# Sixteen attention heads without folded softmax weights, and the sign of 64-bit weights by ScalarE's leaky rectifier

## The chip, the cores and the metric

The kernel runs on one core of a Trainium2 chip. It uses TensorE (PE in the profile), VectorE (DVE), ScalarE (ACT), GpSimd (POOL) and the DMA queue that SyncE (SP) issues. The metric is the device time of one execution in microseconds (us): the median of 3 runs.

## The reference

Three layers follow one another; `rel` is query position minus key position.

```python
# attention: B, H, S, D = 4, 8, 576, 64, window 128
scores = q @ k.T / sqrt(D)
scores = where((rel >= 0) & (rel < 128), scores - slope[h] * abs(rel), -1e9)
attn = softmax(scores);  x = (attn @ v) as [B, S, 512]
# gated layer, d_ff 1024
h = gelu_tanh(x @ w_in);  u, v = halves of h
v_s = w_sg @ (layernorm(v) * g_ln) + b_sg
x = x + (u * v_s) @ w_out
# token-shift layer
xk, xr = mu_k * x + (1 - mu_k) * x_prev, mu_r * x + (1 - mu_r) * x_prev
out = sigmoid(xr @ w_r) * (max(xk @ w_k, 0) ** 2 @ w_v)
```

w_in, w_out, w_k, w_v and w_r come as 64-bit floats; everything else is fp32.

## The kernel before, in words

**Order of work.** There are 32 heads (4 batches of 8). Heads 0 to 7, with the decoding of w_in, come first (slots 0 to 8 of the loop over `slot(n)`). Then each batch's gated layer (`moe1(b)`) is interleaved with the attention of the next batch's heads, by the costs that are written beside the steps: heads 8 to 15 with `moe1(0)`, heads 16 to 23 with `moe1(1)`, heads 24 to 31 with `moe1(2)`. `moe1(3)` runs with the decoding of w_k, and `phase2` is the token-shift layer. All operations are recorded first. A list scheduler with a cost model then gives each engine its fixed order; where an operation has several possible engines ("adp" is ACT, DVE or POOL) it also picks the engine, and tables of offsets (`PRI`, `ENG`) shift priorities. So an operation that vanishes moves others, also from one engine to another.

**A head.** Its 576 queries make 4 tiles of 128 and one of 64. A query tile i sees the key blocks i-1 and i, 256 columns in all, of which the causal window leaves 128 for each query. `s_bank` multiplies queries and keys (tile `s`, PSUM); from head 8 on this takes fp32r copies `QK` of the input `rawqk` and the rest `KL` that they leave. `s_tile` adds bias and mask on DVE (L680, the output `p` and its extreme `nmax`), takes the exponential on ACT (L399), folds, and scales by the reciprocal sum `rin` (L472, L475 or L482, on DVE, POOL or ACT).

**Fold.** Keys outside the window have weight 0 after the exponential. In the key block i-1 the columns right of the diagonal are left, in block i those up to it. `fold(n)` (`n >= FOLD`, FOLD = 0: every head) adds the two 128-column halves into one (`p<-p`, L419 on DVE or L421 on POOL). `tf_step` transposes the four folded tiles in one go (tile `tf`, L385), copies them to `pf` (L407 or L409), and two triangular masks part them again into the two key halves (`keep`: L438 on POOL, L445 on DVE). `tf4_step` does this for the fifth tiles of two heads. `av_step` then multiplies v with the parts (tile `a`).

**64-bit weights.** `job` loads 128 rows of a weight as pairs of 32-bit words. ACT scales the high word in place (`st<-st` or `wraw<-wraw`, L399). On DVE the maximum of that and of its multiple by -2^32 deals with the sign (`wdec<-st` or `wdec<-wraw`, L455); a shift and a merge with the low word follow (L472, L455 with two inputs). The fp32 result `wdec` is split into an fp32r high part (ACT, DVE or POOL) and what it leaves (DVE or POOL). There are 36 such jobs: 8 of w_in, 8 of w_out, 8 of w_k, 4 of w_r, 8 of w_v. `wdec` has 4 buffers for w_in, 2 for w_out, and 1 for w_k, w_r and w_v.

Of the kernel before, what the change touches and what calls it, by code (L numbers as in the profile page):

```python
# [9 lines left out]
F32 = mybir.dt.float32  # L10
# [3 lines left out]
ACTF = mybir.ActivationFunctionType  # L14
ALU = mybir.AluOpType
# [5 lines left out]
P = 128  # L21
# [19 lines left out]
    ("xg", "dve/pool", "dve"): 4000,  # L41
}
NWARM = 10
FOLD = 0
FM = (1, 1)


# [32 lines left out]
class Vw:  # L80
# [25 lines left out]
    def real(self):  # L106
        t = self.base
        if t.real is None:
            t.real = t.rec.open_pool(t.pool).tile(list(t.shape), t.dtype, tag=t.tag, name=t.name, bufs=t.bufs)
        a = t.real  # L110
        for k, x in self.ops:
            if k == "ix":
                a = a[x]
            elif k == "bc":
                a = a.bitcast(x)
            elif x == 3:
                a = a.rearrange("p a b -> p (a b)")
            elif x == 4:
                a = a.rearrange("p a b c -> p (a b c)")
        return a  # L120
# [374 lines left out]
def attn_gmlp_rwkv_kernel(  # L495
# [18 lines left out]
    nc = tc.nc  # L514
    K = Build(nc)
# [11 lines left out]
    def T(pool, shape, dtype, tag, name=None, bufs=None):  # L527
        return R.tile(pool, shape, dtype, tag, name or tag, bufs)

    xs = [T("dr", [P, NC, S + 1], F32, f"xs{b}") for b in range(B)]  # L530
    ident = T("attc", [P, P], F32, "ident")
# [12 lines left out]
    def job(dst_h, dst_l, src, n, dup=False, raw=None, dec=("wraw", "wdec")):  # L544
        if src.dtype != F32:
            if raw is None:
                raw = T(stage[0][0], [P, n, 2], U32, stage[0][1], "wraw")
            K.dma(raw.flat()[:, 0:2 * n], src.bitcast(U32), P * n * 8)
            lo, hi = raw[:, :n, 0], raw[:, :n, 1]
            w = T(dec[0], [P, n], F32, dec[1], "wdec", bufs=4 if dec[0] == "tp" else (2 if dec[0] == "wraw" else 1))  # L550
            wu = w.bitcast(U32)
            hf = hi.bitcast(F32)
            K.act(hf, hf, ACTF.Copy, scale=2.0 ** -112)
            K.stt(w, hf, -(2.0 ** 32), hf, ALU.mult, ALU.max)
            K.ts(wu, wu, 3, None, ALU.logical_shift_left, None)
            K.stt(wu, lo, 29, wu, ALU.logical_shift_right, ALU.bitwise_or, cost=68 + n / 0.96)
        else:
            w = T(stage[0][0], [P, n], F32, stage[0][1], "wraw")
            if dup:
                K.dma(w[0:64], src, 64 * n * 4)  # L560
                K.dma(w[64:128], src, 64 * n * 4)
            else:
                K.dma(w, src, P * n * 4)
        K.copy(dst_h, w, "adp")
        K.sub(dst_l, w, dst_h)
# [8 lines left out]
    def sg_job(kk, half):  # L574
        c = slice(half * HS, half * HS + HS)
        src = w_sgT[kk * P:min(S, kk * P + P), c]
        job(w_sg_t[:, kk, 0, c], w_sg_t[:, kk, 1, c], src, HS, dup=kk == 4)

    def out_job(kk, half):
        c = slice(half * 256, half * 256 + 256)  # L580
        job(w_out_t[:, kk, 0, c], w_out_t[:, kk, 1, c], cols(w_out, kk, half), 256)

    x_t = {}
    NH = B * H
    rawqk, rawv, QK, KL, VS, PT, SUM, PTc = {}, {}, {}, {}, {}, {}, {}, {}

    def plain_s(n):
        return n in PLAIN_S

    def fold(n):  # L590
        return n >= FOLD

    def plain_a(n):
        return n in PLAIN_A
# [114 lines left out]
    def t1_step(n):  # L709
        if fold(n):  # L710
            return tf_step(n)
        t = T("psT", [P, 4, P], F32, "t")
        K.transposes([(t[:, j, :], PT[n, i][:, c:c + P], ident)
                      for j, (i, c) in enumerate(((0, 0), (1, 0), (1, P), (2, 0)))])
        if plain_a(n):
            pf = T("pt", [P, 4, P], F32, "ph1", "pf1")
            K.copy(pf, t)
            PTc[n, 0] = pf
            return
        ph = T("pt", [P, 4, P], F32R, "ph1")  # L720
        pl = T("pt", [P, 4, P], F32R, "pl1")
        K.copy(ph, t)
        K.sub(pl, t, ph)
        PTc[n, 0] = (ph, pl)

    def tf_step(n):

        t = T("psT", [P, 4, P], F32, "t", "tf")
        K.transposes([(t[:, j, :], PT.pop((n, j)), ident) for j in range(4)])
        pf = T("pt", [P, 7, P], F32, "ph1", "pf")  # L730
        if n % FM[0] < FM[1]:
            K.copy(pf[:, 0:4, :], t)
            K.keep(pf[:, 4:7, :], pf[:, 1:4, :], True, "dp")
            K.keep(pf[:, 0:4, :], pf[:, 0:4, :], False, "dp")
        else:
            K.keep(pf[:, 4:7, :], t[:, 1:4, :], True, "d")
            K.keep(pf[:, 0:4, :], t, False, "d")
        PTc[n, 0] = pf

    def tf4_step(n):  # L740
        t = T("psT", [P, 2, 64], F32, "t", "tf4")
        K.transposes([(t[:, j, :], PT.pop((n + j, 4)), ident[:64, :64]) for j in range(2)])
        pf = T("pt", [P, 2, 2, 64], F32, "pf4")
        if n % FM[0] < FM[1]:
            K.copy(pf[:, 0], t)
            K.keep(pf[:, 1], pf[:, 0], True, "dp")
            K.keep(pf[:, 0], pf[:, 0], False, "dp")
        else:
            K.keep(pf[:, 1], t, True, "d")
            K.keep(pf[:, 0], t, False, "d")  # L750
        PTc[n, 1] = pf

    def t2_step(n):
        if fold(n):
            if n % 2:
                tf4_step(n - 1)
            return
        t = T("psT", [P, 4, P], F32, "t")
        o4 = 0 if plain_s(n) else 64
        K.transposes([(t[:, j, :], PT[n, i][:, c:c + P], ident)  # L760
                      for j, (i, c) in enumerate(((2, P), (3, 0), (3, P)))] +
                     [(t[:, 3, 0:64], PT[n, 4][:64, o4:o4 + 128], ident[:64, :64]),
                      (t[:, 3, 64:128], PT[n, 4][:64, o4 + 64:o4 + 192], ident[:64, :64])])
        for i in range(5):
            PT.pop((n, i))
        if plain_a(n):
            pf = T("pt", [P, 4, P], F32, "pl1", "pf2")
            K.copy(pf, t)
            PTc[n, 1] = pf
            return  # L770
        ph = T("pt", [P, 2, P], F32R, "ph2")
        pl = T("pt", [P, 2, P], F32R, "pl2")
        pf = T("pt", [P, 2, P], F32, "pf")
        K.copy(ph, t[:, 0:2, :])
        K.sub(pl, t[:, 0:2, :], ph)
        K.copy(pf, t[:, 2:4, :])
        PTc[n, 1] = (ph, pl, pf)
# [64 lines left out]
    def slot(n):  # L842

        steps = []
        cur, prev = n < NH, n - 1
        has = prev >= 0

        def add(c, f, *a):
            steps.append((c, lambda: f(*a)))
        if cur:  # L850
            add(440, s_bank, n, (0, 1))
        if has:
            add(0, prep_v, prev)
            add(480, t1_step, prev)
        if has:
            add(490, t2_step, prev)
        if cur:
            add(440, s_bank, n, (2, 3))
        if has and prev % 2:
            add(2100, av_step, prev - 1)  # L860
        if cur:
            add(220, s_bank, n, (4,))

            def tail():
                prep_head(n + 1)
                load_head(n + 2)
                load_v(n + 1)
            add(0, tail)
        return steps
# [129 lines left out]
    def phase2(w_k_t):  # L999
# [42 lines left out]
        for kk in range(NC):  # L1042
            job(w_r_t[:, kk, 0, :], w_r_t[:, kk, 1, :], rows(w_r, kk), DM, dec=("raw2", "wdec"))
# [185 lines left out]
```

## Time and profile before

| | |
|---|---|
| median of 3 runs | 627.09 us (625.8 to 627.79) |
| the profiled execution's own time | 628.37 us |
| its span, first to last instruction | 626.6 us |
| mean granted TensorE clock, share of full speed | 0.977 |
| busy: PE, DVE, ACT, POOL | 95%, 76%, 56%, 30% |

Of the columns of the profile: an engine's busy time is followed by the number of its instructions (x). PEclk is the clock granted to TensorE as a share of 2.4 GHz (its lower level, 1.2 GHz, is 0.50). Ends of matmuls are modelled, so a busy PE can still be waiting a little.

### The profile page before, as it was taken

The page shows a single profiled execution, that of the slowest core. Times are in us where ns is not written, and L with a number is a line of the kernel's source. Part 1 is how long each engine was busy: PE and PEld are TensorE (multiplying, and loading weights), DVE is VectorE, ACT ScalarE, POOL GpSimd, SP SyncE. Part 2 cuts the span into 40 slices and gives each one's busy share as a digit, 9 for nine tenths or more (in the row PEclk, how much of TensorE's full clock was granted, in tenths as well). Part 3 has the DMA queues.
Part 4 walks back from the last instruction along what each step waited for, and adds up shares of the span by engine and source line. Part 5 has one row for each costly group of instructions (what it writes and reads, how often), then busy time and mean ns, then how long its engine had stood idle before and what let it go on. Part 6 is the DMA issues. An engine that isn't in the chain of part 4 may idle for free.

```text
span 626.6 us, 10161 instructions
## 1 busy us (share of the span) xinstructions
PE 595.6 (95%) x3458; PEld 498.7 (80%) x3458; DVE 475.6 (76%) x1286; ACT 352.0 (56%) x912; POOL 189.4 (30%) x348
## 2 busy tenths in 40 slices
PE   8776988997999999999999999899999999999997
PEld 4454867895889998899989998688888887888896
DVE  5888799997999998999689999996384229326122
ACT  5988688785798567883337339744330332234031
POOL 5676375432664354642325430000000001000000
PEclk9987999996999999999999999999999999999999
DMA  8961421432513316010081238433002000000100
GB/s 308 311 218 52 141 69 49 154 94 84 170 56 98 97 40 211 21 61 12 1 274 42 97 112 266 129 109 102 33 2 84 18 0 35 33 1 1 52 18 33
DMA packets 25332, 57.74 MB, mean 92 GB/s; under 512 B 4416, under 2 KB 13120, under 8 KB 24768
## 3 DMA queue, kind: packets, MB, share of 16 engines
q1 hardware_dynamic: 25280, 57.09, 27.7%
q8 instruction: 27, 0.44, 0.3%
q14 instruction: 25, 0.20, 0.1%
HBM read 47.63 MB, written 9.45 MB: 91 GB/s over the span
## 4 chain that ended last, share of the span: by engine, by line
PE 76%; DVE 11%; ACT 7%; DMA 3%; issue 2%; POOL 1%; SPq 0%; POOLq 0%; ACTq 0%; DVEq 0%
PE d L377 41%; PE vps L377 16%; PE rps L377 7%; PE s L377 5%; PE a L377 5%; PE tf L385 2%; ACT p L399 2%; DMA rawqk<-in_qk_dram 2%; DVE p L680 2%; DVE wdec L455 1%; DMA wraw<-in_w_r_dram 1%; ACT pf L407 1%; DVE QK L419 1%; ACT p L482 1%; POOL pf L438 1%
## 5 line engine op out<-in xcount | busy, mean ns | idle before, releaser
L377 PE MATMUL d<-xk,wk 128*128 128x512 f32 (+1 forms) x480 | 105.1, 368 | 0.0
L377 PEld LDWEIGHTS d<-xk,wk 128*128 128x128 f32 x480 | 84.7, 188 | 16.0
L377 PE MATMUL vps<-w_v_t,k2h 128*128 128x512 f32 x288 | 93.9, 396 | 0.0
L399 ACT ACTIVATE p<-p,nmax 128x256 f32<-128x256 f32 (+3 forms) x160 | 76.6, 480 | 24.7 <-DVE nmax L680 23.5
L438 POOL TENSOR_SCALAR_AFFINE_SELECT pf<-pf 128x384 f32<-128x384 f32 (+2 forms) x85 | 51.3, 608 | 50.7 <-ACT pf L407 48.5
L680 DVE CUSTOM_DVE_ANT_0 p<-s,mask 128x256 f32<-128x256 f32 (+3 forms) x160 | 59.9, 380 | 8.4 <-PE s L377 8.2
L377 PE MATMUL d<-w_sg_t,vhl 128*128 128x288 f32 x448 | 65.9, 298 | 0.0
L399 ACT ACTIVATE rl<-d 128x512 f32<-128x512 f32 (+1 forms) x40 | 22.1, 554 | 76.3 <-PE d L377 73.4
L377 PEld LDWEIGHTS vps<-w_v_t,k2h 128*128 128x128 f32 x288 | 54.2, 188 | 12.9 <-DVE r L419 0.3
L377 PE MATMUL d<-w_in_t,xg 128*128 128x512 f32 (+1 forms) x240 | 60.9, 402 | 0.3 <-ACT x L407 0.3
L377 PEld LDWEIGHTS d<-w_sg_t,vhl 128*128 128x128 f32 x448 | 60.7, 188 | 0.6 <-issue 0.2
L377 PE MATMUL d<-gg,w_out_t 128*128 128x288 f32 x384 | 56.8, 299 | 3.6 <-DVE gg L419 3.6
L377 PE MATMUL d<-xg,w_in_t 128*128 128x288 f32 x384 | 56.2, 298 | 1.7 <-DVE u L455 1.3
L377 PE MATMUL rps<-w_r_t,xr 128*128 128x512 f32 x216 | 54.6, 392 | 2.8 <-ACT w_r_t L407 1.4
L377 PE MATMUL vps<-w_v_t,k2l 128*128 128x512 f32 x144 | 57.0, 396 | 0.0
L377 PEld LDWEIGHTS d<-gg,w_out_t 128*128 128x128 f32 x384 | 52.5, 190 | 4.7 <-DVE gg L419 3.9
L409 DVE CAST k2h<-rl 128x512 fp32r<-128x512 f32 (+1 forms) x29 | 11.3, 389 | 59.0 <-ACT rl L427 59.0
L377 PEld LDWEIGHTS d<-xg,w_in_t 128*128 128x128 f32 x384 | 52.1, 188 | 3.2 <-DVE u L455 1.8
L377 PEld LDWEIGHTS d<-w_in_t,xg 128*128 128x128 f32 (+1 forms) x240 | 41.8, 180 | 12.4 <-ACT x L407 0.6
L377 PEld LDWEIGHTS rps<-w_r_t,xr 128*128 128x128 f32 x216 | 40.1, 188 | 12.2 <-ACT w_r_t L407 1.9
L419 DVE TENSOR_TENSOR r<-vps,r 128x512 f32<-128x512 f32 x18 | 12.4, 690 | 46.9 <-PE vps L377 46.8
L421 POOL TENSOR_TENSOR p<-p 128x128 f32<-128x128 f32 (+1 forms) x62 | 33.5, 543 | 38.7 <-ACT p L399 32.3
(119 smaller groups left out, 1176.6 us busy)
## 6 DMA issues: line engine op xcount, KB each, us to landing
rawqk<-in_qk_dram SPq DMA_DIRECT2D x32, 576.0 KB, 4.1
rawv<-in_v_dram SPq DMA_DIRECT2D x32, 160.0 KB, 2.7
xs<-x SPq DMA_DIRECT2D x4, 1154.0 KB, 5.3
out_dram<-r SPq DMA_DIRECT2D x18, 256.0 KB, 2.0
st<-in_w_in_dram SPq DMA_DIRECT2D x8, 512.0 KB, 7.1
wraw<-in_w_k_dram SPq DMA_DIRECT2D x8, 512.0 KB, 3.8
wraw<-in_w_v_dram SPq DMA_DIRECT2D x8, 512.0 KB, 3.5
wraw<-in_w_out_dram SPq DMA_DIRECT2D x8, 256.0 KB, 2.6
```

Of the source, the lines that this page charges most:

```text
L377: pe.matmul(real(o), real(l), real(r), start=st, stop=sp, **ex)
L385: pe.transpose(real(o), real(i), real(d))
L399: nc.scalar.activation(real(out), real(in_), func, scale=scale, **kw)
L407: alts.append(("act", self._act(in_), lambda: nc.scalar.copy(real(out), real(in_))))
L409: alts.append(("dve", self._dve(in_.n, not in_.ps), lambda: nc.vector.tensor_copy(real(out), real(in_))))
L419: alts.append(("dve", self._dve(out.n, False), lambda: nc.vector.tensor_tensor(real(out), real(a), real(b), op)))
L421: alts.append(("pool", 140 + 2.12 * out.n, lambda: nc.gpsimd.tensor_tensor(real(out), real(a), real(b), op)))
L438: nc.gpsimd.affine_select(out=real(out), in_=real(in_), pattern=[[0, rows], [sgn, n]], compare_op=cmp, fill=0.0, base=0, channel_multiplie ...
L455: alts.append(("dve", cost or self._dve(out.n, False, isinstance(s, Vw)), lambda: nc.vector.scalar_tensor_tensor(real(out), real(a), real( ...
L482: alts.append(("act", self._act(a, 1), lambda: nc.scalar.mul(real(out), real(a), real(s1))))
L680: K.raw("dve", 70 + w / 0.96, lambda: nc.vector.tensor_tensor_reduce(out=real(pw), in0=real(si), in1=real(ma), scale=-0.125, scalar=3.0e38 ...
```

## The change

Three things change. FOLD is 16, so heads 0 to 15 take the other path that `t1_step` and `t2_step` have had all along: no fold and no masks; the scaled 128x256 tiles are transposed in both key halves, as four 128x128 transposes in `t1_step` and three 128x128, two 64x128 and (new) one 64x64 in `t2_step`, each group copied whole to its half of one tile `pf1`. The maximum that deals with the sign of a 64-bit weight goes from DVE into the activation that scales: a leaky rectifier (Prelu) whose slope for negative values is -2^32, and whose output is `wdec` and no longer the loaded words.

```diff
-FOLD = 0
+FOLD = 16
...
-            K.act(hf, hf, ACTF.Copy, scale=2.0 ** -112)
-            K.stt(w, hf, -(2.0 ** 32), hf, ALU.mult, ALU.max)
+            K.raw("act", K._act(hf), lambda: nc.scalar.activation(
+                real(w), real(hf), ACTF.Prelu, scale=2.0 ** -112, alpha=-(2.0 ** 32)), [hf], [w])
             K.ts(wu, wu, 3, None, ALU.logical_shift_left, None)
...
         if plain_a(n):
-            pf = T("pt", [P, 4, P], F32, "ph1", "pf1")
-            K.copy(pf, t)
-            PTc[n, 0] = pf
+            PF[n] = T("pt", [P, 8, P], F32, "ph1", "pf1")
+            K.copy(PF[n][:, 0:4], t)
+            PTc[n, 0] = PF[n][:, 0:4]
             return
...
                      (t[:, 3, 64:128], PT[n, 4][:64, o4 + 64:o4 + 192], ident[:64, :64]),
+                      (t[:64, 3, 64:128], PT[n, 4][:64, o4 + 128:o4 + 192], ident[:64, :64])])
...
         if plain_a(n):
-            pf = T("pt", [P, 4, P], F32, "pl1", "pf2")
+            pf = PF.pop(n)[:, 4:8]
             K.copy(pf, t)
             PTc[n, 1] = pf
             return
```

The scheduler writes a new order. Three places of it follow. On TensorE, among the first heads, this stood before (`s` is a score product, `tf` a transpose of folded weights, `a` the product with v):

```order
L385 MATMUL tf<-ident,p 128x128 x4
L377 MATMUL s<-rawqk 128x128
L377 MATMUL s<-rawqk 128x256 x3
L385 MATMUL tf<-ident,p 128x128 x4
L377 MATMUL s<-rawqk 64x192
L385 MATMUL tf_304<-ident,p 128x64 x2
L377 MATMUL s<-rawqk 128x128
```

In the changed program, from the first transpose on (`t` is a transpose of weights that were not folded):

```order
L385 MATMUL t<-ident,p 128x128 x4
L377 MATMUL s<-rawqk 128x128
L377 MATMUL s<-rawqk 128x256
L385 MATMUL t<-ident,p 128x128 x3
L385 MATMUL t<-ident,p 128x64 x2
L385 MATMUL t<-ident,p 64x64
L377 MATMUL s<-rawqk 128x256 x2
L377 MATMUL s<-rawqk 64x192
```

A head now has ten transposes in two groups, where two heads had ten in three.

On GpSimd, where the first tiles of `moe1(0)` begin (`mv` is a layer norm's statistics), this stood before:

```order
L438 AFFINE_SELECT pf<-pf 128x384
L438 AFFINE_SELECT pf<-pf 128x512
L438 AFFINE_SELECT pf_1040<-pf_1040 128x128
L475 TENSOR_SCALAR mv<-mv 128x1
L916 TENSOR_TENSOR mv<-mv,mhalf 128x1
L438 AFFINE_SELECT pf_1040<-pf_1040 128x128
L421 TENSOR_TENSOR p<-p 128x128
L917 TENSOR_SCALAR mv<-mv 128x1
```

And in the changed program:

```order
L421 TENSOR_TENSOR KL<-rawqk,QK 128x576
L421 TENSOR_TENSOR w_sg_t<-wraw,w_sg_t 128x288
L475 TENSOR_SCALAR mv<-mv 128x1
L917 TENSOR_TENSOR mv<-mv,mhalf 128x1
L918 TENSOR_SCALAR mv<-mv 128x1
L475 TENSOR_SCALAR p<-p,rin 128x256 x2
```

The masks and the folds are gone here, and a `KL` has come over from VectorE. All 24 `KL` stood on VectorE; now 10 do, and 14 stand on GpSimd: 6 of them ahead of the first fold of head 16, 8 behind it.

On TensorE, at the start of `phase2` (`d<-xk,wk` is the product with w_k, `rps` that with w_r, `vps` that with w_v), this stood before:

```order
L377 MATMUL d<-gg,w_out_t 128x288 x90
L377 MATMUL d<-xk,wk 128x512 x90
L377 MATMUL rps<-w_r_t,xr 128x512 x6
L377 MATMUL d<-xk,wk 128x512 x6
L377 MATMUL rps<-w_r_t,xr 128x512 x42
```

And in the changed program:

```order
L377 MATMUL d<-xk,wk 128x512 x66
L377 MATMUL rps<-w_r_t,xr 128x512 x6
L377 MATMUL d<-xk,wk 128x512 x12
L377 MATMUL rps<-w_r_t,xr 128x512 x6
L377 MATMUL d<-xk,wk 128x512 x12
L377 MATMUL rps<-w_r_t,xr 128x512 x6
L377 MATMUL d<-xk,wk 128x512 x6
L377 MATMUL rps<-w_r_t,xr 128x512 x12
```

The first products with w_r have moved ahead of 24 products with w_k. Both programs load ScalarE's activation table twice, once at the start and once ahead of the first sigmoid.

## Rows read from the trace of the kernel before

**Rows 1.** Busy time of each engine in four stretches (--windows); x: instructions.

```profile
0.00:160.00 160.00, 135.79 (x825) 104.10 (x825) 139.50 (x439) 123.73 (x368) 87.43 (x169) 0.91 0.45 146
160.00:390.00 230.00, 229.93 (x1596) 206.21 (x1595) 211.35 (x553) 148.65 (x392) 97.73 (x174) 1.00 0.32 104
390.00:400.00 10.00, 8.03 (x33) 5.68 (x32) 9.86 (x22) 7.00 (x12) 0.00 (x0) 1.00 0.49 151
400.00:627.00 227.00, 221.88 (x1008) 182.75 (x1008) 114.91 (x276) 72.67 (x144) 4.23 (x5) 1.00 0.12 40
```

**Rows 2.** The same by 8 us: PE, PEld, DVE, ACT, POOL, PEclk, DMA share, GB/s.

```profile
8.00:16.00 8.00, 6.20 (x28) 3.83 (x28) 7.47 (x38) 7.80 (x30) 4.33 (x9) 1.00 1.02 398
...
24.00:32.00 8.00, 6.05 (x28) 3.50 (x30) 7.56 (x32) 7.75 (x26) 5.36 (x10) 1.00 0.94 315
...
40.00:48.00 8.00, 6.64 (x25) 4.90 (x27) 6.65 (x25) 5.83 (x21) 5.62 (x11) 0.57 0.63 203
...
56.00:64.00 8.00, 6.67 (x26) 3.81 (x25) 5.86 (x17) 5.92 (x18) 6.57 (x12) 0.50 0.11 30
...
144.00:152.00 8.00, 6.65 (x28) 5.02 (x30) 7.25 (x24) 4.74 (x17) 2.28 (x4) 0.50 0.22 75
```

**Rows 3.** Chain of work that ended last: start us, us, what.

```profile
29.82 1.43 ACT p L399 x6
...
45.29 3.01 PE a L377 x14
...
58.48 0.70 POOL pf L438
...
136.77 5.17 DMA rawqk<-in_qk_dram
...
159.75 0.44 PE tf L385 x4
...
300.64 0.44 PE tf L385 x4
302.66 0.26 PE tf L385 x2
...
310.87 1.66 PE a L377 x16
```

**Rows 4.** Groups by shape: count | busy us, mean ns of one | idle before.

```profile
L455 DVE SCALAR_TENSOR_TENSOR wdec<-st 128x512 f32<-128x512 f32 x8 | 7.7, 962 | 0.4 <-ACT st L399 0.4
L455 DVE SCALAR_TENSOR_TENSOR wdec<-wraw 128x256 f32<-128x256 f32 x8 | 4.9, 609 | 0.0
L399 ACT ACTIVATE st<-st 128x512 f32<-128x512 f32 x8 | 5.4, 670 | 0.0
L421 POOL TENSOR_TENSOR p<-p 128x128 f32<-128x128 f32 x43 | 25.6, 598 | 31.7 <-ACT p L399 25.6 <-PE a L377 4.1 <-PE d L377 1.0
L419 DVE TENSOR_TENSOR p<-p 128x128 f32<-128x128 f32 x53 | 18.7, 356 | 3.2 <-ACT p L399 2.6
L438 POOL TENSOR_SCALAR_AFFINE_SELECT pf<-pf 128x512 f32<-128x512 f32 x31 | 23.7, 767 | 1.5
L407 ACT COPY pf<-tf 128x512 f32<-128x512 f32 x30 | 17.4, 579 | 7.1 <-PE tf L385 6.9
L482 ACT ACTIVATE p<-p,rin 128x128 f32<-128x128 f32 x89 | 30.5, 393 | 7.5 <-DVE rin L703 7.0
L407 ACT CAST w_out_t<-wdec 128x256 fp32r<-128x256 f32 x8 | 3.2, 405 | 1.9 <-DVE wdec L455 1.8
L421 POOL TENSOR_TENSOR w_in_t<-wdec,w_in_t 128x512 fp32r<-128x512 f32 x2 | 2.9, 1426 | 1.7 <-ACT w_in_t L407 1.7
```

**Rows 5.** The same, of the first 160 us alone.

```profile
L399 ACT ACTIVATE p<-p,nmax 128x256 f32<-128x256 f32 x54 | 27.2, 505 | 2.9 <-DVE nmax L680 2.2 <-DVE sum L472 0.3
L419 DVE TENSOR_TENSOR KL<-rawqk,QK 128x576 fp32r<-128x576 f32 x11 | 8.5, 774 | 0.0
```

**Rows 6.** PE's own waits (engine, line, waited for: us in total, times, longest).

```profile
PE s L377 <- DVE nmax L680: 10.8, 12, 2.4
PE d L377 <- DVE gg L419: 3.6, 1, 3.6
PE a L377 <- POOL pf L438: 3.4, 5, 1.3
PE s L377 <- DVE KL L419: 1.8, 2, 1.5
PE rps L377 <- ACT w_r_t L407: 1.4, 1, 1.4
PE rps L377 <- ACT r L399: 1.2, 1, 1.2
```

**Rows 7.** Start of `phase2` in order of time: start us, us, instructions.

```profile
379.62 11.04 PE L377 MATMUL d<-xk,wk 128*128 128x512 f32 x48
390.50 1.52 PE L377 MATMUL rps<-w_r_t,xr 128*128 128x512 f32 x6
...
396.86 0.73 PE L377 MATMUL rps<-w_r_t,xr 128*128 128x512 f32 x2 [1.44 <-ACT w_r_t L407]
```

More of the change, by code (lines that the diff above doesn't have):

```diff
@@ L584, in attn_gmlp_rwkv_kernel @@
     NH = B * H
-    rawqk, rawv, QK, KL, VS, PT, SUM, PTc = {}, {}, {}, {}, {}, {}, {}, {}
+    rawqk, rawv, QK, KL, VS, PT, SUM, PTc, PF = {}, {}, {}, {}, {}, {}, {}, {}, {}
     def plain_s(n):
@@ L762, in t2_step @@
                      [(t[:, 3, 0:64], PT[n, 4][:64, o4:o4 + 128], ident[:64, :64]),
-                      (t[:, 3, 64:128], PT[n, 4][:64, o4 + 64:o4 + 192], ident[:64, :64])])
+                      (t[:, 3, 64:128], PT[n, 4][:64, o4 + 64:o4 + 192], ident[:64, :64]),
+                      (t[:64, 3, 64:128], PT[n, 4][:64, o4 + 128:o4 + 192], ident[:64, :64])])
         for i in range(5):
```

## The prediction

> **What bounds the kernel now.** I read the stretches first, since a share over the whole span hides the stage. From 160 to 390 us TensorE is busy 229.9 of 230 us, and from 400 us to the end it idles 5.1 us; only before 160 us, and around 390 us, does it wait [rows 1]. So work that is saved on another engine is worth something in those two places alone. The first 160 us hold the 16 heads that change, heads 0 to 7 and then 8 to 15 with `moe1(0)`: head 16's transposes stand at 159.75 us [rows 3]. There TensorE idles 24.2 us and its clock is 0.91 of full [rows 1], a further 14 us if that clock were always what holds things up.
>
> The finer stretches show which engine leads. Early on VectorE and ScalarE are both nearly full, 7.5 and 7.8 of 8 us. Later TensorE falls to 1.2 GHz for stretches (0.50 at 56 and at 144 us, 0.57 at 40 us) [rows 2]. TensorE's own waits say whom it waits for: the scores' evictions on VectorE (10.8 us), `gg` (3.6), the masks on POOL (3.4), `KL` (1.8) [rows 6]. The chain of work runs over ScalarE's exponentials early, over POOL's masks at 58 us, and over a late load of `rawqk` at 137 us [rows 3]. It is therefore a stage in which VectorE leads (139.5 of 160 us), ScalarE follows (123.7), and latencies between them do the rest [rows 1].
>
> **VectorE in the first 160 us.** The sign pass goes: 8 of 0.962 us for w_in and 8 of 0.609 us for w_out, 12.6 us [rows 4]. Of the folds, 64 of 128 vanish; in the new order VectorE has 28 fewer of the 128-column ones, 28 x 0.356 = 10.0 us [rows 4], and I leave out the small ones. Six `KL` move to POOL, 6 x 0.774 = 4.6 us [rows 5]. That is 27 us. Against it the new order gives VectorE five wide scalings, three of the copies out of PSUM and some twelve casts, sums and evictions that stood elsewhere. At 0.4 to 0.6 us, from the scaling to the copy of [rows 4], these 20 take back 8 to 12 us. I take 9: VectorE falls by 18, to 121.5 us.
>
> **ScalarE.** Each head now copies two 512-column tiles out of PSUM. ScalarE has 29 of those 32 where it had 16: 13 x 0.579 = 7.5 us more [rows 4]. Scalings get wider, but 57 narrow ones go (57 x 0.393 = 22.4 us) and 29 wide ones come. A wide one isn't in the trace; below it lies the narrow one (0.393 us) [rows 4] and above it the exponential over the same 256 columns (0.505) [rows 5], so 11.4 to 14.6 us; I take the upper, as the width is the same: 7.8 us less. About 15 casts move to other engines, at 0.405 us 6 us [rows 4]. ScalarE ends some 6 to 7 us lower, at 117 us, but none of that comes early: in the lead-in the copies come and the exponentials stay.
>
> The rectifier itself isn't in the trace. Its lower bound is the scaling pass whose place it takes, 0.670 us; its upper bound is that plus the whole pass it replaces, 1.63 us [rows 4]. I take the lower, since it is the same engine over the same 512 words with one output; it then takes the scaling's place at no cost. With the upper, 16 passes would add up to 15 us to ScalarE and use up the gain.
> The Trainium skill (ScalarE: Activation LUTs, What ACT_TABLE_LOAD costs) states that an activation runs at one element per cycle whatever its function; by it the rectifier would cost what the scaling cost. No run here shows it yet.
>
> **POOL.** It loses 15 or 16 of each kind of large mask (0.767 us for the wider) and 20 large folds (0.598 us) [rows 4] and gains wide scalings and 14 `KL`. It was idle for 73 of 160 us [rows 1], so its sum matters less than what it delays. What it gives up lies between a transpose and the product with v, where two masks in a row stood on the chain (0.70 us) [rows 3]: that latency is gone.
>
> **TensorE.** A head's transposes grow from four and one small to seven and three small. Four cost 0.44 us and two small ones 0.26 [rows 3], so 3 x 0.11 + 2 x 0.13 = 0.59 us, and 9.4 us for 16 heads. All of it falls before 160 us. Its cover is the 24.2 us that TensorE idles there [rows 1]; where a stretch becomes TensorE's, it costs its full price.
>
> **Sum of the stage.** If VectorE kept its share of the stretch (139.5 of 160), 121.5 us of work would need 139 us: 21 us gained. If ScalarE kept its share (123.7 of 160), 117 us would need 151: 9 us gained. TensorE's idle time less its new work leaves 24.2 - 9.4 = 15 us as the most that waits can give. I choose 9.5, near ScalarE's figure, because ScalarE's early load is what does not shrink.
>
> **After 160 us.** From 160 to 390 us nothing is gained, whatever gets lighter [rows 1]. At 390 us `phase2` starts and TensorE waits 1.4 us for `w_r_t` and 1.2 for the first sigmoid [rows 6]. VectorE loses 12 sign passes of w_k and w_r ahead of this place, but `wdec` has one buffer there, so a job's rectifier now waits on ScalarE, in front of whatever is queued there, until the job before has been split. And the new order asks for w_r 24 products earlier: 48 products take 11.04 us [rows 7], so 5.5 us earlier. Either the lighter VectorE has decoded w_r by then, or TensorE waits up to that long. I book 0, with 3 us gained and 5.5 lost as ends.
>
> The profiled execution has a span of 626.6 us and its own time is 628.37, 0.2% above the median of 627.09. Median less 9.5 is **617.5 us**.
>
> **Rivals.**
> *VectorE was the whole bound.* Then the stage gains what TensorE leaves, 15 us, and a little clock: 611 us. VectorE's 87% of the stretch [rows 1] speaks for it, ScalarE's 7.8 of 8 us early [rows 2] against it.
> *ScalarE holds the lead-in.* Its exponential chain (six pieces in 1.43 us without a gap) [rows 3] has no less to do, and with the copies more; only heads 8 to 15 gain, about half: 622.5 us. The early rows of ScalarE speak for it; that it is busy only 5.8 and 5.9 of 8 us at 40 and 56 us [rows 2] speaks against.
> *w_r is late.* The stage gains as forecast and `phase2` loses 5.5: 623 us. For it: the wait for `w_r_t` that is there already [rows 6]. Against: VectorE's load, 9.9 of 10 us there [rows 1], falls.
> *The other side: KL on POOL.* A `KL` by POOL should take 1.426 x 576 / 512 = 1.60 us [rows 4] in place of 0.774 [rows 5], behind whatever POOL does. The score products wait for it, and TensorE's order is fixed. Eight of the 14 lie behind the first fold of head 16, where TensorE has no slack [rows 1]. If those come late by 1.2 us each or more, 9.6 us are lost and the gain is gone; at 2 us each the time is 634 us. For it: `KL` on VectorE was already waited for [rows 6]. Against: POOL is free for more than half of 160 to 390 us.
> The Trainium skill (GPSIMD Engine Reference, 4.1 Engine selection) sends elementwise work on whole tiles to VectorE, since GpSimd is about twice as slow on two inputs. By that rule the moved `KL` are a loss, at an estimated 2 x 0.774 = 1.55 us each; the scheduler's choice goes against it, and the trace has no `KL` on POOL to decide.
> *The clock.* TensorE falls to 1.2 GHz after sparse stretches [rows 2]; there a product group with v took 3.01 us for 14 pieces against 1.66 for 16 at full clock [rows 3]. Three such groups more, with scores and transposes between, cost some 6 us: 623.5 us. Against it, TensorE has more to do than before.
> *The rectifier is slow,* or is no gain to anybody: 627 us or a little more.
>
> **How the numbers follow.** Chances: forecast 0.42; VectorE the whole bound 0.15; ScalarE holds the lead-in 0.17; w_r late 0.06; the clock 0.06; KL on POOL 0.10; slow rectifier 0.04. The forecast's own range is 613 to 621. To hold 8 in 10, the range reaches down to 608 (the second case with clock) and up to 625.5, past the three that end near 623, and leaves out KL and the slow rectifier and the outer parts. A change within 0.3% (1.9 us) is about what a measurement of this kernel can't tell from none. Faster by more: the first five less a little, 0.80. Same: 0.07, from the upper ends of the lead-in case and the weaker forms of the last two. Slower: 0.13.
>
> **What would show it.** In the new profile: VectorE near 120 us and TensorE's idle time near 15 us up to head 16's transpose, which should come near 150 us where it stood at 160; scaling passes of about 0.67 us under the name `wdec` on ScalarE; TensorE full from there to `phase2`. Wrong would be: TensorE waits for `KL` from POOL after that point; a rectifier near 1 us or more; a third table load; a wait of several us for `w_r_t`; or a lead-in as long as before with ScalarE full.

## The result, and the profile after

The changed kernel takes 618.63 us (median of 4 runs, 616.41 to 620.08) where the kernel before takes 626.44 (4 runs beside it, 624.51 to 627.79): a ratio of 0.9875, with an interval of 0.9834 to 0.9915. It is faster by 7.8 us. Forecast were 617.5 us, in a range of 608 to 625.5. Times and medians here are of runs in the chip's faster state; one run of e11 below (665.02 us) fell in the slower one and is left out.

The profiled execution took 618.84 us by itself, with a span of 616.9. Busy time by stretches in the changed kernel (start:end, length, then PE, PEld, DVE, ACT and POOL with their instructions, granted clock, DMA share, GB/s), to be held against [rows 1]:

```profile
0.00:150.00 150.00, 135.56 (x901) 110.19 (x902) 122.47 (x392) 119.18 (x333) 73.35 (x132) 0.93 0.48 160
...
160.00:380.00 220.00, 217.78 (x1530) 195.49 (x1529) 199.06 (x505) 138.73 (x360) 101.07 (x175) 1.00 0.30 97
380.00:400.00 20.00, 19.74 (x87) 15.93 (x86) 17.48 (x39) 12.95 (x23) 0.00 (x0) 1.00 0.51 162
400.00:617.00 217.00, 212.97 (x969) 174.96 (x968) 101.85 (x240) 66.50 (x132) 11.12 (x17) 1.00 0.10 35
```

The first stage now ends near 150 us. In it VectorE is busy 122.5 us, ScalarE 119.2, and TensorE idles 14.4. From 160 to 380 us TensorE idles 2.2 us, where it idled 0.1 from 160 to 390 us in [rows 1]. Around the start of `phase2` (380 to 400) it idles 0.3 us; before, it idled 2.0 in 10 us [rows 1].

The chain of work of the changed kernel, at four places (start us, us, what):

```profile
63.57 2.75 PE a L377 x16
66.32 0.67 PE s L377 x4
66.99 1.40 PE d L377 x6
...
87.65 0.44 PE t L385 x4
...
90.74 0.65 PE t L385 x6
...
148.65 0.44 PE tf L385 x4
```

Head 16's transposes stand at 148.65 us, 11.1 earlier than in [rows 3]. The first product with w_in (`d`, near 67 us) is 3.7 us later than before (63.2 by the trace); ahead of it now stand 40 more transposes, 8 more score products and 8 more products with v (these write tiles that are also named `s`). The two parts of the stage, in the kernel before and then in the changed one (columns as above):

```profile
0.00:64.00 64.00, 48.61 (x230) 29.70 (x231) 51.28 (x182) 49.72 (x155) 43.37 (x86) 0.87 0.66 219
64.00:150.00 86.00, 77.18 (x526) 66.43 (x526) 80.33 (x232) 67.26 (x191) 40.95 (x78) 0.96 0.31 98
```

```profile
0.00:64.00 64.00, 49.55 (x268) 33.96 (x270) 44.97 (x160) 49.41 (x144) 33.89 (x65) 0.85 0.69 235
64.00:150.00 86.00, 86.00 (x636) 76.23 (x633) 77.50 (x233) 69.77 (x190) 39.47 (x67) 0.99 0.33 104
```

From 64 to 150 us TensorE idled 8.8 us at 0.96 of its clock; now it idles nothing at 0.99. So the lead-in, up to the first product with w_in, gives nothing back, and the gain stands between 67 and 149 us.

What TensorE itself waits for in the changed kernel, against [rows 6]:

```profile
PE s L377 <- DVE nmax L680: 4.8, 7, 2.4
PE t L385 <- POOL p L475: 2.8, 2, 2.0
PE t L385 <- ACT p L482: 2.6, 1, 2.6
PE d L377 <- DVE u L455: 2.0, 3, 0.9
PE s L377 <- ACT pf L407: 1.5, 3, 0.7
```

The waits for the scores' evictions have more than halved (10.8 before). Those for `gg` (3.6), for POOL's masks (3.4), for `KL` (1.8) and for `w_r_t` (1.4) are gone. Waits for scalings, on POOL and ScalarE, ahead of the transposes have grown from 1.1 to 5.4 us.

The prices, from the groups by shape (count | busy us, mean ns of one | idle before):

```profile
L553 ACT ACTIVATE wdec<-st 128x512 f32<-128x512 f32 x8 | 5.2, 661 | 0.0
L553 ACT ACTIVATE wdec<-wraw 128x512 f32<-128x512 f32 x20 | 13.4, 672 | 11.0 <-DVE w_v_t L419 4.3 <-DMA wraw<-in_w_k_dram 3.2 <-DVE wk L419 2.6
L482 ACT ACTIVATE p<-p,rin 128x256 f32<-128x256 f32 x21 | 10.2, 504 | 2.4 <-DVE rin L703 2.4
L421 POOL TENSOR_TENSOR KL<-rawqk,QK 128x576 fp32r<-128x576 f32 x14 | 21.3, 1519 | 13.7 <-issue 7.0 <-ACT QK L407 5.9 <-POOL sum L675 0.7
L419 DVE TENSOR_TENSOR KL<-rawqk,QK 128x576 fp32r<-128x576 f32 x10 | 8.7, 876 | 0.0
L399 ACT ACT_TABLE_LOAD x2 | 2.6, 1283 | 0.8 <-PEq L1217 0.8
```

The leaky rectifier costs what the scaling cost that it replaces (661 and 672 ns against 670 in [rows 4]); the idle time in its second row belongs to the jobs of w_k, w_r and w_v, where ScalarE has room. The table is still loaded twice.

**Where the 9.7 us of span come from.** Head 16's transposes come 11.1 us earlier. About 2.1 us of this is only order: from there to the first product with w_k TensorE has 212.5 us of work where it had 210.4. So the stage gained 9.0. In the same stretch 2.1 us are lost (idle 2.2 against 0.1; the waits for `u` on VectorE are 2.0). From the first product with w_k to the end it takes 253.7 us, against 256.6: 2.8 gained. These are the two profiled executions; that of the kernel before took 1.9 us more than the median of its runs, so by the medians the change is worth 7.8.

### The profile page after: what moved, and what is told of

It is laid out like the page before. It is cut to its first block, busy times and chain, and to the rows that moved or that the text cites. A ratio compares the mean times of both kernels' runs of the same rounds, so it can differ in the third digit from the quotient of the medians.

```text
span 616.9 us, 10182 instructions
## 1 busy us (share of the span) xinstructions
PE 596.0 (97%) x3538; PEld 505.0 (82%) x3538; DVE 450.3 (73%) x1204; ACT 343.9 (56%) x868; POOL 191.6 (31%) x334
## 4 chain that ended last, share of the span: by engine, by line
PE 85%; DVE 8%; ACT 4%; issue 1%; DMA 1%; POOL 1%; SPq 0%; ACTq 0%; DVEq 0%; POOLq 0%
PE d L377 47%; PE vps L377 16%; PE s L377 7%; PE rps L377 6%; PE a L377 5%; PE t L385 3%; ACT p L399 1%; PE tf L385 1%; DVE p L680 1%; DVE wdec L455 1%; ACT pf L407 1%; DMA rawqk<-in_qk_dram 1%; DVE QK L419 1%; DVE gt L455 1%; ACT wdec L553 0%
## 5 line engine op out<-in xcount | busy, mean ns | idle before, releaser
L475 POOL TENSOR_SCALAR p<-p,rin 128x128 f32<-128x128 f32 (+4 forms) x63 | 35.3, 570 | 35.9 <-DVE rin L703 27.3
L482 ACT ACTIVATE p<-p,rin 128x128 f32<-128x128 f32 (+4 forms) x86 | 33.3, 429 | 8.3 <-DVE rin L703 8.2
```

What stands on the lines that cost most here:

```text
L475: alts.append(("pool", 240 + out.n if ptr else 150 + 0.83 * out.n, lambda: nc.gpsimd.tensor_scalar(real(out), real(a), real(s1), real(s2), ...
L482: alts.append(("act", self._act(a, 1), lambda: nc.scalar.mul(real(out), real(a), real(s1))))
```

## The experiments

The table has, for every kernel, the median, its ratio to the kernel before on the same chip with the interval, and four times of the profiled execution in us from the start of its span: first product with w_in, head 16's first transpose, first product with w_k, end. The kernel before had medians of 626.27 beside e1 to e4, 626.76 beside e5 to e8, and 625.85 beside e9 to e12.

| kernel | median | ratio (95%) | w_in | head 16 | w_k | end |
|---|---|---|---|---|---|---|
| before | 626.44 | 1 | 63.2 | 159.6 | 370.1 | 626.6 |
| after | 618.63 | 0.9875 (0.9834 to 0.9915) | 66.8 | 148.5 | 363.2 | 616.9 |
| e1 unfolding alone | 614.58 | 0.9800 (0.9763 to 0.9837) | 61.1 | 146.6 | 357.4 | 613.6 |
| e2 rectifier alone | 619.76 | 0.9883 (0.9844 to 0.9923) | 72.7 | 155.0 | 366.2 | 619.2 |
| e3 after, all `KL` on VectorE | 616.17 | 0.9824 (0.9788 to 0.9860) | 64.5 | 148.2 | 358.7 | 613.8 |
| e4 after, only heads 8 to 15 unfolded | 619.85 | 0.9893 (0.9842 to 0.9944) | 71.6 | 156.5 | 365.7 | 618.7 |
| e5 after, rectifier only for w_k, w_r, w_v | 613.46 | 0.9783 (0.9756 to 0.9809) | 61.6 | 148.7 | 359.0 | 612.4 |
| e6 e2, w_sg held back | 623.85 | 0.9954 (0.9934 to 0.9973) | 68.5 | 154.5 | 368.7 | 621.7 |
| e7 after, all 32 heads unfolded | 625.10 | 0.9976 (0.9951 to 1.0000) | 66.8 | 148.4 | 370.2 | 624.8 |
| e8 after, w_sg held back | 615.91 | 0.9833 (0.9803 to 0.9862) | 65.0 | 150.9 | 362.5 | 616.7 |
| e9 e1's order, rectifier | 611.39 | 0.9766 (0.9743 to 0.9788) | 59.5 | 145.0 | 355.4 | 611.0 |
| e10 before's order, rectifier | 623.06 | 0.9943 (0.9917 to 0.9969) | 59.5 | 152.5 | 363.1 | 618.7 |
| e11 before, `KL` on POOL | 626.99 | 1.0012 (0.9994 to 1.0031) | 66.1 | 156.6 | 367.5 | 623.7 |
| e12 before, another order | 626.07 | 0.9989 (0.9969 to 1.0008) | 67.0 | 156.4 | 368.4 | 626.1 |

**e1 and e2: each part alone.** e1 keeps the old sign pass; e2 keeps the fold.

```diff
 (e1)
-            K.raw("act", K._act(hf), lambda: nc.scalar.activation(
-                real(w), real(hf), ACTF.Prelu, scale=2.0 ** -112, alpha=-(2.0 ** 32)), [hf], [w])
+            K.act(hf, hf, ACTF.Copy, scale=2.0 ** -112)
+            K.stt(w, hf, -(2.0 ** 32), hf, ALU.mult, ALU.max)
 (e2)
-FOLD = 16
+FOLD = 0
```

> Heads 0 to 15 without fold, the sign pass as before on VectorE. The changed kernel's trace gains 11.1 us up to head 16's transposes, loses 2.6 us until the start of phase 2 and gains about 2.8 us there (first product with w_v 14.7 us earlier, end 9.7 us earlier). Theory 'the unfolded heads give the stage its gain, the rectifier gives phase 2 its gain': 619 to 622 us here, head 16's transposes at 150 to 153 us, the wait for w_r_t at the start of phase 2 (2.6 us) still there. Rival 'the rectifier's 12.6 us on VectorE are what the stage gained': 624 to 627 us and head 16 at 156 to 160 us.

> All heads folded as before, only the rectifier is new. Theory 'unfolded heads give the stage its gain': head 16's transposes at 156 to 160 us, but phase 2 starts without its 2.6 us wait, so 623 to 625 us. Rival 'VectorE's relief of 12.6 us in the first 160 us is what counts': head 16 near 150 us and 616 to 620 us.

The unfolding alone gains 11.7 us, more than the whole change (7.8) and more than either case on record had for e1. The rectifier alone gains 6.5: its total fits the rival of e2 (616 to 620 us), but head 16, at 155.0, stands close to the theory's 156 to 160. Added to the unfolding the rectifier takes 4 us back (614.58 to 618.63; the two intervals only touch), and the unfolding added to the rectifier gains 1.1 (619.76 to 618.63; not resolved). So the parts don't add up. In e2 the first product with w_in comes 9.5 us late, at 72.7, behind 4 more score products and 8 more products with v. Its chain of work there:

```profile
26.69 7.79 DMA rawv<-in_v_dram
34.50 3.24 DMA wraw<-in_w_sgT_dram
...
40.49 2.07 POOL w_sg_t L421 x2
42.56 0.94 POOL pf L438
43.56 1.18 POOL pf L438
...
46.45 2.08 DMA wraw<-in_w_sgT_dram
48.56 0.43 ACT w_sg_t L407
```

The new order draws more of the work on w_sg, a weight that is needed only later, into the lead-in (20 of its splitting steps stand ahead of the first product with w_in, where the kernel before has 15), some of it in front of POOL's masks, and POOL takes about 1 us for each step.

**e3: `KL` back on VectorE.**

```diff
-            K.sub(kl, raw[:, 1, :], q[:, 1, :])
+            K.sub(kl, raw[:, 1, :], q[:, 1, :], "d")
```

> The changed kernel with all 24 KL kept on VectorE (14 of them stood on GpSimd). In the kernel before, the stretch from 132 to 160 us held a late load of rawqk (5.2 us on the chain) that waits for a KL on VectorE, and half clock behind it; the changed kernel gains 9 us in just that stretch. Theory 'KL on GpSimd frees the buffer in time': the late load and its loss come back, 624 to 628 us, head 16 near 157 us. Rival 'VectorE's lighter load does it, wherever KL stands': 616 to 620 us, head 16 at 147 to 151 us, and the 2.6 us lost between 230 and 310 us (if KL on GpSimd causes them) come back.

The interval of e3 (0.9788 to 0.9860) overlaps that of the changed kernel (0.9834 to 0.9915), so the 2.5 us between them are not resolved. The theory that `KL` on POOL makes the gain (624 to 628 us) fell. The prediction's rival, a loss of 9.6 us or more by `KL` on POOL, did not come either: the changed kernel has no wait of TensorE for `KL` at all, though each costs POOL 1519 ns. A loss of a few us isn't excluded.

**e4, e6 and e8: why is the lead-in late?** e4 unfolds heads 8 to 15 only and keeps the rectifier. e6 (on e2) and e8 (on the changed kernel) let the loads of w_sg be placed only after the first batch's last `xg`.

```diff
 (e4)
-        return n >= FOLD
+        return not 8 <= n < FOLD
 (e6, e8: this load and the two of half a tile)
-                K.dma(w, src, P * n * 4)
+                K.dma(w, src, P * n * 4, [XG[0][:, 3, 1, :]])
```

> Only heads 8 to 15 are unfolded; heads 0 to 7 keep fold and masks. In the changed kernel the first product with w_in comes 3.7 us later than before (66.8 for 63.2 us). Theory 'unfolding costs the lead-in time, through wider scalings, more copies on ScalarE and more transposes, and pays only beside the gated layer': first product at 60 to 63 us and 613 to 617 us in all. Rival 'the lead-in's loss comes from the rectifier or from the new order': first product at 65 to 68 us and 618 us or more.

> All heads folded, rectifier everywhere, and the ten loads of w_sg held back in the scheduler until the last xg of batch 0 is split. With the rectifier alone the first product with w_in came at 72.7 us (63.2 before), and the chain there runs over loads of w_sg and v (3.2 and 7.8 us) and over splits of w_sg on GpSimd with the masks queued behind. Theory 'w_sg, drawn into the lead-in, is what holds it': first product at 61 to 65 us; of the 8 to 11 us won there at least half lasts, 611 to 617 us. Rival 'the rectifier itself makes the lead-in slow (its place on ScalarE, its output buffer)': first product at 70 to 74 us, and 619 to 623 us.

> The changed kernel with the loads of w_sg held back in the same way (6 fewer KL end up on GpSimd). Theory 'w_sg in the lead-in': first product with w_in at 61 to 64 us (66.8 in the changed kernel) and 611 to 616 us. Rival: first product at 66 us or later, or the work on w_sg comes due too late and TensorE waits for it near 110 us: 618 us or more.

e4 has the lead-in of e2 (71.6 against 72.7), with its first eight heads folded; the idea that the first heads' unfolding makes the lead-in late fell. Holding w_sg back moves the first product from 72.7 to 68.5 in e2 and from 66.8 to 65.0 in the changed kernel. That is 4.2 of 9.5 us, and 1.8 of the 5.7 by which the changed kernel is behind e1: at most a part of the cause (e8 also has 6 fewer `KL` on POOL). And e6 loses what it won there, and more, later (623.85 against 619.76), while e8 can't be told from the changed kernel (intervals overlap).

Two more things are in the table. Held against e2, e4 shows no gain from unfolding heads 8 to 15 beside the rectifier: 619.85 against 619.76, and head 16 at 156.5 against 155.0. And the two parts of the stage can't be judged apart: e2, with every head folded, has a lead-in 9.5 us longer than before, but takes 82.3 us from the first product with w_in to head 16, where the kernel before takes 96.4 and the changed kernel 81.7.

**e5: the rectifier only for w_k, w_r and w_v.** The order of TensorE up to `phase2` is then that of e1.

```diff
+            if dec[0] == "raw2":
                 (the rectifier)
+            else:
+                (the old scaling and sign pass)
```

> Heads 0 to 15 unfolded; the rectifier only for w_k, w_r and w_v, the old sign pass for w_in and w_out, so TensorE's order up to phase 2 is that of the run with unfolded heads alone. There the span from the first product with w_k to the end was 256.2 us, and with the rectifier 253.0 to 253.7. Theory 'the rectifier is worth about 3 us at the start of phase 2 and costs the lead-in time through the order': 610 to 612.5 us, phase 2 253 to 254 us. Rival 'its gain there came from the other order of phase 2 alone or from elsewhere': 613.5 to 616 us.

The first product with w_in is at 61.6, as in e1, and the median (613.46) stands between the two cases, at the rival's edge. From the first w_k product to the end it takes 253.4 us where e1 takes 256.2; but head 16's transposes came 2.0 us later than in e1, at the same TensorE order, and the totals (613.46, 614.58) overlap. One execution's time of a place is thus good to about 2 us at best. The gain in `phase2` seems to go with a rectifier that the order was remade for: 253.0 to 254.7 us there in e2, e4 to e8 and the changed kernel (e3: 255.1), but 255.6 and 255.7 in e9 and e10 and 256.2 in e1. The changed kernel's own `phase2` in order of time (start us, us, instructions), against [rows 7]:

```profile
364.77 13.54 PE L377 MATMUL d<-xk,wk 128*128 128x512 f32 x59
378.15 1.52 PE L377 MATMUL rps<-w_r_t,xr 128*128 128x512 f32 x6
379.51 2.88 PE L377 MATMUL d<-xk,wk 128*128 128x512 f32 x12
382.23 1.52 PE L377 MATMUL rps<-w_r_t,xr 128*128 128x512 f32 x6
```

The products with w_r stand between those with w_k, and none has to wait.

**e7: all 32 heads unfolded.**

```diff
-FOLD = 16
+FOLD = 32
```

> All 32 heads unfolded. Heads 16 to 31 lie where TensorE is full. Theory 'there a head's five added transposes cost their whole price, 0.53 to 0.59 us (0.44 + 0.65 us a head now, 0.44 + 0.13 before)': 16 x 0.52 = 8.4 us more, 625 to 629 us, against 618.6. Rival 'the lighter GpSimd and VectorE give it back': 617 to 621 us.

It measured 625.10, as the theory had it and 6.5 us above the changed kernel for 16 more unfolded heads. Their transposes stand in its chain at full price:

```profile
202.42 0.44 PE t L385 x4
...
203.13 0.65 PE t L385 x6
```

A head then costs 1.09 us of transposes; folded, two heads cost 0.44 + 0.44 + 0.26 = 1.14 [rows 3], 0.57 each. So 0.52 us a head, 8.3 for 16. TensorE is busy 220.0 of 220 us from 160 to 380 there; what it saves in waits for `u` (2.0 in the changed kernel, none here) takes the 8.3 to 6.3.

**e9 and e10: the rectifier without a new order.** The rectifier writes in place of the scaling, in all 36 jobs, and VectorE's 36 sign passes are planned but not issued, so every engine keeps the order of e1 (e9) or of the kernel before (e10). The shift reads the loaded words. Nothing of the computation is left out.

```diff
-            K.act(hf, hf, ACTF.Copy, scale=2.0 ** -112)
-            K.stt(w, hf, -(2.0 ** 32), hf, ALU.mult, ALU.max)
-            K.ts(wu, wu, 3, None, ALU.logical_shift_left, None)
+            K.raw("act", K._act(hf), lambda: nc.scalar.activation(
+                real(hf), real(hf), ACTF.Prelu, scale=2.0 ** -112, alpha=-(2.0 ** 32)), [hf], [hf])
+            K.raw("dve", K._dve(n, False), lambda: real(w), [hf, hf], [w])
+            K.raw("dve", K._dve(n, True), lambda: nc.vector.tensor_scalar(
+                real(wu), real(hi), 3, None, ALU.logical_shift_left), [wu, hi], [wu])
```

> Heads 0 to 15 unfolded, and the rectifier in all 36 jobs, in place on the loaded words, while the scheduler still plans with the old sign pass: every engine has the order of the run with unfolded heads alone (614.6 us, first product with w_in at 61.1 us), only without VectorE's 36 passes; the shift reads the loaded words. Theory 'the rectifier itself does no harm, what the lead-in lost is the new order': first product at 59 to 62 us, phase 2 some 2 to 3 us shorter, 609 to 613 us. Rival 'ScalarE's rectifier or the lost pass as such slows the lead-in': first product at 64 us or later and 615 to 619 us.

> All heads folded and the order of every engine as before, only that VectorE's 36 sign passes are gone (rectifier in place, the shift reads the loaded words). Theory 'VectorE's load is what the first 160 us wait for, as the prediction's sum has it': 12.6 us less of it gain 6 to 10 us up to head 16's transposes and 2 to 3 us in phase 2, 615 to 619 us. Rival 'the order has to change for the relief to count, since the engines wait for each other and not for VectorE's sum': at most 3 us in the stage, 621 to 625 us.

e9 is the best version, 611.39 us (610.65 to 612.96), ahead of both kernels. With the order kept, the rectifier gains some 3 us on either base: e10 is 2.8 below the kernel before (by its interval 1.9 to 5.2), and e9 is 14.5 below it where e1 is 11.7 below, though the intervals of e9 and e1 overlap. Of the 2 to 3 us expected in `phase2`, 0.7 and 0.9 came.

The trace of e10 says more than its median: head 16 comes at 152.5, 7.0 us earlier than before, inside the 6 to 10 us of the theory. But that execution took 620.38 us, 2.7 below the median of its runs, and the kernel before's was above its own. The eight runs of e10 go from 619.3 us at a mean clock of 0.991 to 625.46 at 0.975, so the median and its interval decide here, and the total lies in the rival's range (621 to 625). The first 160 us of e10, and what TensorE waits for in them:

```profile
0.00:160.00 160.00, 138.03 (x866) 106.16 (x866) 137.43 (x446) 128.97 (x386) 89.63 (x178) 0.95 0.48 157
```

```profile
PE s L377 <- DVE nmax L682: 9.5, 12, 2.4
PE a L377 <- POOL pf L438: 3.8, 6, 1.2
PE d L377 <- DVE gg L419: 2.6, 1, 2.6
PE s L377 <- DVE KL L419: 1.5, 1, 1.5
```

VectorE's stage is without 12.6 us of sign passes [rows 4]. Its busy time up to head 16 falls by less, by 8.9 us, here before and in e10; the shift that now reads the loaded words takes 432 ns over 128x256 where it took 291.

```profile
0.00:159.58 159.58, 135.38 (x820) 103.68 (x821) 139.08 (x439) 123.31 (x367) 87.12 (x169) 0.91 0.45 146
```

```profile
0.00:152.54 152.54, 130.57 (x820) 99.69 (x821) 130.14 (x423) 122.88 (x366) 84.20 (x169) 0.94 0.47 153
```

TensorE's waits are nearly those of [rows 6], entry by entry: 9.5 us for evictions where it was 10.8, 3.8 for masks where it was 3.4. In e1 the wait for masks is gone and that for evictions is 3.8 us:

```profile
PE s L377 <- DVE nmax L680: 3.8, 7, 1.1
```

What the remade order does to the lead-in is seen beside e9. Three stretches of 8 us of the changed kernel, then of e9 (columns as in the first table of stretches):

```profile
24.00:32.00 8.00, 5.48 (x27) 3.61 (x25) 6.54 (x25) 7.36 (x26) 4.42 (x7) 0.77 0.95 314
32.00:40.00 8.00, 7.80 (x45) 6.32 (x46) 5.43 (x14) 6.28 (x16) 3.18 (x7) 0.80 0.64 180
40.00:48.00 8.00, 5.64 (x22) 3.36 (x22) 6.90 (x23) 6.11 (x19) 5.38 (x8) 0.62 0.34 112
```

```profile
24.00:32.00 8.00, 6.10 (x38) 4.14 (x40) 5.88 (x24) 7.87 (x25) 4.53 (x6) 1.00 0.90 307
32.00:40.00 8.00, 6.42 (x45) 4.31 (x41) 6.00 (x23) 7.68 (x24) 3.98 (x9) 1.00 0.79 242
40.00:48.00 8.00, 6.82 (x51) 4.95 (x50) 5.37 (x20) 7.77 (x26) 6.96 (x11) 1.00 0.65 206
```

In e9 ScalarE is kept at 7.7 to 7.9 of 8 us and TensorE stays at 2.4 GHz; in the changed kernel ScalarE has gaps and the granted clock falls to 0.62. Over the first 64 us the clock is 0.85 there and 0.95 in e9, which is some 6 us of full clock, near the 7.3 us between their first products with w_in (the changed kernel has four score products more ahead of it). The gaps and the clock go together; which of the two came first these runs don't tell. e9 differs from the changed kernel in writing in place too, not in the order alone; but ScalarE's waits for the single buffer of `wdec`, in the rows of prices above, belong to the jobs of w_k, w_r and w_v, and w_in has four buffers.

**e11 and e12: two controls on the kernel before.** e11 puts `KL` of heads 8 to 15 on POOL, e12 changes only a bias of the scheduler, which gives another order.

```diff
 (e11)
-            K.sub(kl, raw[:, 1, :], q[:, 1, :])
+            K.sub(kl, raw[:, 1, :], q[:, 1, :], "p" if n < 16 else "dp")
 (e12)
-    BIAS_DP, BIAS_DA, BIAS_AP = 3000.0, 1500.0, 1500.0
+    BIAS_DP, BIAS_DA, BIAS_AP = 2500.0, 1500.0, 1500.0
```

> The kernel before with the eight KL of heads 8 to 15 on GpSimd. Theory 'the late load of rawqk at 137 us, and the half clock behind it, come from a KL that stands late on VectorE': the loss of some 9 us between 132 and 160 us goes, 617 to 621 us. Rival 'KL's place is not the cause': 624 to 629 us.

> A control: the kernel before with one number of the scheduler changed (the bias between VectorE and GpSimd, 2500 for 3000), so the same work stands in another order. If the order before was an ordinary one, the time stays within 3 us of 626.5. If it was an unlucky one, above all between 132 and 160 us, other orders of the same work come out at 615 to 622 us, and part of the gain of the change is not its own.

Neither changes the median. In both traces the late load of `rawqk` at 137 us [rows 3] is gone from the chain and head 16 stands 3 us earlier, and yet the medians don't move: the late load was one shape of the stage's loss, not its cause, and 3 us in a place of one trace need not be a gain. With e11 the theory fell that `KL` on VectorE cost the stage time before.

## Why the prediction held, point by point

**The stage: right in size.** Forecast were 9.5 us of gain, with VectorE near 120 us, ScalarE at 117, TensorE's idle time near 15, and head 16 near 150. Measured were 9.0, 122.5, 119.2, 14.4 and 148.5. That the gain came so near is in good part luck: head 16 comes 13.0 us earlier than before in e1, 11.1 in the changed kernel and 4.6 in e2, and what the remade orders cost or give was no term of the sum.

**The measure behind the size: this step failed.** The prediction let the stage shrink with an engine's share: 21 us by VectorE's, 9 by ScalarE's. In e10, at an unchanged order, VectorE's busy time up to head 16 falls by 8.9 us; by its share in [rows 1] that alone would give 8.9 x 160 / 139.5 = 10.2. The whole program gained 2.8 by the medians, at most 5.2 by the interval (the two traces have 7.0 up to head 16). So by the medians VectorE's share gives about twice too much, or more. ScalarE's figure came out near the result, but not for the reason given, that its early load doesn't shrink. That load indeed stayed (49.4 us busy in the first 64 us, 49.7 before), and the lead-in got no shorter; yet ScalarE wasn't full, and e9, with 51.6 us of ScalarE work in the same stretch, has its first w_in product 7.3 us earlier than the changed kernel. What the stage seems to be made of are handovers in a fixed order: scores to evictions, exponentials to scalings, transposes to copies to masks to products with v. The unfolding takes links out of that chain (folds, masks, and a group of transposes that waits for two heads). It is worth 11.7 us alone, and it removes the waits for masks and most of those for evictions; the rectifier only lightens an engine and gains 3 at the same order. That the removed links, rather than the removed folding work on VectorE and POOL, are what pays is not shown: it was not tried apart, and the order counts as much. At the orders of e9 and e10 the unfolding is worth 11.7 us beside the rectifier as well, but only 1.1, not resolved, between e2 and the changed kernel, whose orders were remade for the rectifier.

**The lead-in: half of a named sign came.** "A lead-in as long as before with ScalarE full" was listed as what would speak against the forecast; the lead-in was that long, and ScalarE had gaps. It is 3.7 us longer to the first w_in product. The 40 transposes more (0.52 us a head, 4.2 for eight heads) are about that size, but they aren't the reason: e1 has the same 40 ahead of that product and reaches it at 61.1 us, 2.1 earlier than the kernel before. The rival by which ScalarE holds the lead-in was wrong in its engine. It was right in that the gain stands behind the lead-in; that heads 8 to 15 earn it is not shown (e4 against e2). Against e1 the remade order's lead-in is 5.7 us longer, and 7.3 against e9. Why stays open (holding w_sg back gives 1.8 of the 5.7, no more than two executions of one order differ by).

**TensorE's price: right.** 0.59 us a head was forecast, 0.52 measured; e7 shows that it is paid in full where TensorE is full. In the stage it was covered: the unfolding alone gains there.

**The unknown prices.** The rectifier was taken at its lower bound, 0.670: 0.661 and 0.672. The wide scaling on ScalarE was taken at the upper bound, 0.505: 0.504. The Trainium skill (ScalarE: Activation LUTs, What ACT_TABLE_LOAD costs) has an activation run at one element per cycle whatever its function; by these rows the trace agrees. `KL` on POOL was put at 1.60 and costs 1.519. The Trainium skill (GPSIMD Engine Reference, 4.1 Engine selection) puts GpSimd at about twice VectorE's time on two inputs. The traces agree: 1519 ns against 876 in the changed kernel, a factor of 1.7, and 1428 against 759 in e1, 1.9. Whether the 14 `KL` on POOL are a loss is not resolved: TensorE waits for none of them, and e3 without them is 2.5 us lower with overlapping intervals.

**After 160 us.** "Nothing is gained" held, but 2.1 us were lost to waits for `u`, which had no place in the sum. `phase2` was booked at 0 with 3 us of gain as one end; it gained 2.8, and the waits for `w_r_t` (1.4) and for the first sigmoid (1.2) are gone. The two cancel but for 0.7 us.

**The clock** had a chance of 0.06, for 6 us lost. Against the kernel before it isn't lower (0.93 up to 150 us, 0.92 there). Against e9 (0.98) it is, in the lead-in, so a low clock goes with what the remade order costs.

## What to carry to other kernels

Where every engine has a fixed order and each waits for the others, a share of busy time of 87% is no bound: expect little from work saved on one engine (here 2.8 us in all for 8.9 saved in the stage alone), and look, though these runs only argue for it, at which handovers an edit removes from the chain. When a scheduler remakes the order after an edit, the new order is an edit of its own, worth several us of either sign: measure the edit once at the old order, by leaving the vanished instructions planned but not issued, and keep whichever order is better.

Work that moves onto a full engine costs its price, and the same work where that engine idles can be covered: unfolding 16 heads gained 11.7 us, unfolding the next 16 lost 6.5.

## What the runs showed of the hardware that was not expected

A leaky rectifier with a scale, over every second 32-bit word of 512 pairs, takes ScalarE no longer than the plain scaled copy (661 to 679 ns against 669 to 682), and needed no further table load beside the exponential's and the sigmoid's (2 loads of 1283 ns, as before).

TensorE's granted clock in one and the same stage can differ by how the work is ordered: 0.77, 0.80 and 0.62 from 24 to 48 us in the changed kernel, 1.00 throughout in e9, which has the same work of TensorE ahead of its first product with w_in but for four score products. Over the whole span the clock is 0.982 to 0.991 in the changed kernel's four runs and 0.992 to 0.994 in e9's five.
